# Signs of 64-bit weights masked as 32-bit words into a tile of marks, in an order made anew

## The chip, the cores and the metric

One core of a Trainium2 chip runs the whole program. The metric is its device time in microseconds (us). The engines are named as in the profile: PE (TensorE, matmuls), PEld (its weight loads), DVE (VectorE), ACT (ScalarE), POOL (GpSimd) and SP (SyncE, which issues the DMAs).

## What is computed

An attention with gates over 768 positions (2 batches, 8 heads of 40), as a recurrence; its output, 1536 tokens of 320, goes through a first layer with 64-bit weights, and then through 8 experts:

```
m_new = np.maximum(f_gate[:, :, t] + m, i_gate[:, :, t])
C = f_stab * C + i_stab * einsum('bhd,bhe->bhde', vt, kt)   # and n likewise
y[:, :, t] = o * (C q) / maximum(|n q|, 1)
...
h = x @ w_in                  # 320 x 2048, float64
g = np.maximum(0.01 * h, h)
x = (g @ w_out).astype(np.float32)     # 2048 x 320, float64
...
out += P[:, e:e + 1] * (np.maximum(x @ w1[e], 0.0) @ w2[e])   # 8 experts
```

## The kernel before

**Three stages.** The attention is worked in chunks of 128 positions with matmuls (six pairs, `c0` to `c5`, and more behind). The first layer runs over steps g: a block of 256 tokens by 128 hidden columns. Step g has an up product `u` (8 matmuls, L223), a leak `g` (ACT, L712), a rounded part `h` (ACT, L718), the remainder `l` (DVE, L723, tile `hla`) and a down product `d` (6 matmuls, L230 to L232). The experts follow.

**The 64-bit weights.** They arrive as pairs of 32-bit words and are turned into two fp32 parts on the chip. There are 16 loads n = 0 to 15: an even n is 768 columns of `w_in`, an odd n 640 columns of `w_out`. Each goes through these steps, named with their n: `L` the DMA (L158); `pa` the sign (L193, DVE): the top bit is taken from byte 7 of a pair and put in byte 3; `pl` three low bits (ACT L187 or DVE L185); `pu` a scaling of the high word (ACT L178 or DVE L176), which shifts the exponent's bias; `pb` the join (L199, DVE): the high word moved left by 3 and or-ed with the low word; `ph` the rounded part (ACT, L211); `px` the remainder, called a low here (L215, DVE or POOL). The raw words lie in four buffers: `rawU` for n % 4 = 3 and three `raws`, so load n+4 waits for the low of load n.

**What sets the order.** Up to the end of step 31 and the chunks c0 to c5, every engine's order is that of a table, `ORDER`: a list of task names that one loop runs through, each task issuing its instructions on its engines. `VECTORED` names the `pu` and `pl` that go to DVE instead of ACT, `POOLED` the tasks that go to POOL instead of DVE. Beside the steps the table has the chunks' tasks, `c1.xl` for instance: `bd` (L559) spreads the gates for a decay product, `ap0` and `ap1` are the decay products (L566, L568), `sc` the scores (L591), `wg` and `kw` weigh (L597, L602), `va` the values (L607), `zp` the product with the state (L613), `dp` the update of the state (L619) with its rows of decay (L475), `cr` carries it on (L660 to L665), `zt`, `ya`, `dn`, `sg`, `ou` make the chunk's output (L624 to L643), `tt`, `xi`, `xl` turn it into columns for PE (L335 to L345). `wN` stands for N dummy matmuls whose result isn't read (L881); 20 more of them run at the start (L899). The gates' scans (L412, L424) and what follows them (to L441) come first on DVE. From step 32 on, the order is that of the program's loops, and is not the table's.

Of the kernel before, what the change touches and what calls it, by code (L numbers as in the profile page):

```python
# [31 lines left out]
nT@0 c1.qP f2 ex c0.bd og0 pl3 L2 pu3 c2.q3 f4 w8@p c0.ap0@1 n8 c1.v c1.ap1@2 n5 f3 c1.kn w1@p c1.ap0@3 n9 c0.ex0 pa3  # L32
c0.ap1@1 n7 c0.sc c0.ex1 pb3 c1.ex0 c2.bd qT@1 c1.ex1 c0.wg pu1 pl1 w8@p c0.va@3 nS c0.kw ph3 pa1 qTe pl0 px3 c0.dp@2
pb1 pu0 c1.sc c0.cr nTe ph1 pa0 nL@1 px1 c2.ap1@0 nLe sg0 pb0 c3.ap1@2 L5 c2.kP c4.bd c0.dn c2.qP c1.wg c2.v c2.kn L7
pu2 c0.sg c3.kP c0.ou c2.ex1 c1.kw w13@h c0.tt@1 pl2 c1.va@3 qS pa2 c0.xi ph0 pb2 w3@h c1.dp@0 c3.ex1 px0 c0.xl pl5
c2.ap0@2 c1.cr qL@1 c2.ex0 c1.dn c2.zp@0 pu5 c1.sg L4 c2.kw c3.ap0@2 qLe c1.ou c3.q3 ph2 c2.zt c3.qP c1.tt@1 pa5 c3.kn
c2.sc@30 c1.xi px2 c3.ex0 c1.xl f6 w1@h c2.dp@2 c2.wg c4.kP u0 L6 c2.cr pu4 c2.va@1 c3.v pu7 pb5 g0 c4.ap0@0 h0 c3.kw
c2.ya u1 f5 l0 c2.dn c4.ap1@3 g1 d0 pl4 pl7 pa4 c3.zp@2 c4.ex0 h1 u2 c2.sg c4.q3 pu6 l1 c4.qP pb4 c3.sc@10 c4.v g2
c4.ex1 c4.kn pa7 ph4 u3 c2.ou h2 c3.wg px4 d1 g3 h3 l2 c3.dp@3 pl6 c2.tt@0 ph5 c4.kw L8 c3.va@1 c3.cr og4 c2.xi l3 u4
pa6 u5 c3.zt g4 pb7 d2 pb6 ph7 c4.zp@3 h4 px5 ph6 d3 px7 l4 L9 c2.xl g5 c4.dp@2 h5 c3.ya pu8 d4 px6 L11 pl8 c5.kn  # L40
c4.sc@01 c4.af c3.dn L10 sg4 l5 u6 c3.sg c4.wg c5.kP c5.qP d5 c5.q3 c3.ou pa8 u7 g6 pu11 c4.zt c3.tt@0 g7 c4.va@1
c3.xi h6 c3.xl h7 pl11 l6 pb8 c5.ap1@3 c5.v c5.ap0@0 c5.ex1 u8 l7 c4.ya d6 pa11 g8 u9 pu10 h8 pb11 ph8 d7 l8 c5.ex0
c4.dn c5.sc@13 g9 c4.sg e7 c5.af h9 u10 pl9 l9 c5.kw d8 ph11 px8 u11 px11 c5.wg c5.dp@0 g11 g10 d9 h11 L15 pl10 l11
L12 c5.va@1 c4.ou h10 pu9 l10 pa9 u12 pb9 c5.zp@3 pa10 g12 ph9 d10 h12 px9 u13 l12 L13 pu12 d11 g13 pb10 h13 d12 pu15
l13 pl15 ph10 u14 c5.zt px10 u15 g14 h14 L14 d13 l14 g15 f8 h15 u16 pa15 pl12 l15 pu13 d14 c5.ya g16 pb15 u17 h16 l16
c5.dn d15 g17 pl14 h17 u18 pu14 l17 c5.sg pa12 u19 g18 h18 pl13 d16 pb12 g19 l18 d17 h19 l19 u20 pa14 u21 pa13 g20
# [1262 lines left out]
```

## Time and profile before

| | |
|---|---|
| Time, median of 3 runs | 936.43 us (936.31 to 936.45) |
| The profiled execution | 936.21 us, of which the span is 934.5 |
| PE busy | 926.1 us, 99% of the span |
| DVE, ACT, POOL busy | 587.2, 490.3, 553.0 us |
| First up product (u0) begins | 33.40 us |
| First step behind the table (u32) begins | 112.23 us |

The span is the time from the profile's first instruction to its last; 1.7 us of the execution's time lie outside of it. Busy time of PE includes the dummy matmuls, and a matmul's duration includes its way through the array, so that those of successive ones overlap.

### The profile page before, as it was taken

The numbers are of one execution on the slowest core, as the hardware profiler recorded it, in microseconds if no ns is written. First come the engines' busy times: TensorE is split into PE (matmuls) and PEld (weight loads), VectorE is DVE, ScalarE is ACT, GpSimd is POOL, SyncE is SP. The second block draws the span as 40 slices with busy tenths as digits, with TensorE's granted clock in tenths as the row PEclk, the third lists the DMA queues.
The fourth block names the chain that finished last, engine by engine and source line by source line (L and its number), as shares of the span: only waits on it lengthen the run. The fifth ranks groups of instructions, "written<-read, shape, count | busy, mean of one in ns | idle before, by whom it ended". The sixth has DMA issues, their size and how long they took to land.

```text
span 934.5 us, 16892 instructions
## 1 busy us (share of the span) xinstructions
PE 926.1 (99%) x6192; PEld 904.7 (97%) x6192; DVE 587.2 (63%) x1179; ACT 490.3 (52%) x959; POOL 553.0 (59%) x575
## 2 busy tenths in 40 slices
...
GB/s 272 247 214 151 24 105 35 67 23 17 88 2 46 33 41 34 43 52 38 38 38 44 51 40 51 38 38 38 45 50 43 48 38 38 38 47 50 29 2 84
DMA packets 57384, 56.49 MB, mean 60 GB/s; under 512 B 7654, under 2 KB 48086, under 8 KB 57302
## 3 DMA queue, kind: packets, MB, share of 16 engines
...
q14 instruction: 34, 0.28, 0.1%
...
## 4 chain that ended last, share of the span: by engine, by line
PE 92%; DVE 3%; DMA 2%; ACT 1%; issue 1%; SPq 1%; POOL 0%; DVEq 0%; ACTq 0%
PE y L230 12%; PE y L231 12%; PE y L232 12%; PE ha L223 9%; PE b L1028 8%; PE b L1029 8%; PE b L1031 8%; PE b L1030 8%; PE ya L230 3%; PE ya L232 3%; PE ya L231 3%; PE yps L607 1%; PE sps L591 1%; PE zps L613 1%; DMA rawU<-in_w_out_dram 1%
## 5 line engine op out<-in xcount | busy, mean ns | idle before, releaser
L1052 POOL TENSOR_TENSOR hl<-c,hh 128x384 fp32r<-128x384 f32 x192 | 197.4, 1029 | 180.1 <-ACT c L1051 156.3
L230 PE MATMUL y<-w_e,hh 128*128 128x320 f32 x768 | 238.4, 310 | 0.0
L231 PE MATMUL y<-w_e,hh 128*128 128x320 f32 x768 | 236.9, 308 | 0.0
L232 PE MATMUL y<-w_e,hl 128*128 128x320 f32 x768 | 236.8, 308 | 0.0
L1110 DVE SCALAR_TENSOR_TENSOR acc<-y,Pg,acc 128x320 f32<-128x320 f32 x336 | 179.1, 547 | 63.6 <-PE y L232 56.3
L1050 ACT ACTIVATE hh<-c 128x384 fp32r<-128x384 f32 x192 | 99.8, 520 | 208.1 <-DVE c L1047 208.1
L1028 PE MATMUL b<-X,w_e 128*128 128x384 f32 x448 | 152.7, 341 | 0.2 <-DVE s L1068 0.2
L1029 PE MATMUL b<-X,w_e 128*128 128x384 f32 x448 | 151.0, 337 | 0.0
L1031 PE MATMUL b<-X,w_e 96*128 96x384 f32 x448 | 151.0, 337 | 0.0
L1030 PE MATMUL b<-X,w_e 128*128 128x384 f32 x448 | 150.8, 337 | 0.0
L230 PEld LDWEIGHTS y<-w_e,hh 128*128 128x128 f32 x768 | 144.2, 188 | 1.7 <-DVE acc L1108 1.1
L231 PEld LDWEIGHTS y<-w_e,hh 128*128 128x128 f32 x768 | 144.3, 188 | 0.0
L232 PEld LDWEIGHTS y<-w_e,hl 128*128 128x128 f32 x768 | 144.1, 188 | 0.0
L1051 ACT ACTIVATE c<-c 128x384 f32<-128x384 f32 x192 | 101.0, 526 | 18.0 <-ACT hh L1050 0.7
L223 PE MATMUL ha<-xT,w_a 128*128 128x256 f32 x768 | 109.2, 286 | 1.0 <-DVE hla L723 1.0
L1047 DVE TENSOR_TENSOR c<-b,s 128x384 f32<-128x384 f32 x192 | 100.6, 550 | 13.5 <-PE b L1031 10.1
L223 PEld LDWEIGHTS ha<-xT,w_a 128*128 128x128 f32 x768 | 101.0, 192 | 2.5 <-DVE hla L723 1.4
L1075 DVE SCALAR_TENSOR_TENSOR hl<-b,hh 128x384 fp32r<-128x384 f32 x64 | 35.6, 557 | 95.4 <-ACT hh L1074 95.4
L723 POOL TENSOR_TENSOR hla<-gg,hha 128x256 fp32r<-128x256 f32 x64 | 48.8, 763 | 78.0 <-ACT hha L718 71.0
L259 POOL TENSOR_TENSOR raw_e<-raw_e 128x256 f32<-128x256 f32 x116 | 85.1, 743 | 4.5
L1028 PEld LDWEIGHTS b<-X,w_e 128*128 128x128 f32 x448 | 84.8, 189 | 1.3 <-DVE s L1068 0.6
L1029 PEld LDWEIGHTS b<-X,w_e 128*128 128x128 f32 x448 | 85.2, 190 | 0.0
...
## 6 DMA issues: line engine op xcount, KB each, us to landing
...
rawU<-in_w_out_dram SPq DMA_DIRECT2D x4, 640.0 KB, 5.0
...
raws<-in_w_out_dram SPq DMA_DIRECT2D x4, 640.0 KB, 3.8
```

Source lines behind the costliest of these rows:

```text
L223: nc.tensor.matmul(h_ps, t1[:, ws, c * P:(c + 1) * P], xt[:, xs, t0:t0 + n], start=(j == 0), stop=(j == len(MM1) - 1),)
L230: nc.tensor.matmul(y_ps, a, t2[:, c, :], start=first, stop=False)
L231: nc.tensor.matmul(y_ps, a, t2[:, 2 + c, :], start=False, stop=False)
L232: nc.tensor.matmul(y_ps, b, t2[:, c, :], start=False, stop=last)
L1028: nc.tensor.matmul(bank, f[:, 0], b[:, 0], start=fresh, stop=False, skip_group_check=not fresh)
L1029: nc.tensor.matmul(bank, f[:, 0], b[:, 2], start=False, stop=False, skip_group_check=not fresh)
L1030: nc.tensor.matmul(bank, f[:, 2], b[:, 0], start=False, stop=False, skip_group_check=not fresh)
L1031: nc.tensor.matmul(bank, f[0:K3, 1], b[0:K3, 1], start=False, stop=True, skip_group_check=not fresh)
L1047: nc.vector.tensor_tensor(c, part, plus, op=ALU.add)
L1051: nc.scalar.activation(c, c, AF.Relu)
L1052: nc.gpsimd.tensor_tensor(hl[a][b], c, hh[a][b].bitcast(F32), op=ALU.subtract)
L1110: nc.vector.scalar_tensor_tensor(out=o, in0=y, scalar=Pg[:, 2 * HP * q + t, e:e + 1], in1=o, op0=ALU.mult, op1=ALU.add)
```

## The change

The sign is now an and of the whole high word with the top bit, from every second 32-bit word of the raw buffer into a contiguous tile of marks (`late`). The low bits are written behind it, as bytes into the lowest byte of each mark, so that `pa` stands ahead of `pl`, where `pl` stood ahead of `pa`. The join reads the marks in place of the low words. There is one tile of marks for even n and one for odd n, so the sign of load n+2 follows the join of load n. Two later uses share the memory of `late`: the leaked tiles of steps from 32 on, and the copies of `repeat`. Three steps that stood in the loops behind the table are now its last: `c6.bd`, `xr` (`repeat`) and `xl` (an expert's first load). `VECTORED`, `POOLED` and `ORDER` are new throughout; of `ORDER` the first line stands here.

```diff
-VECTORED = ('pl2', 'pl4', 'pu9', 'pu10', 'pu12', 'pl14', 'pl15')
-POOLED = ('c1.kw', 'c2.bd', 'c2.kw', 'c3.kw', 'c3.sg', 'c4.bd', 'c4.sg', 'px0', 'px2', 'px4', 'px7', 'px11')
+VECTORED = ('pu4', 'pu6', 'pu7', 'pl9', 'pu12', 'pu13', 'pl13', 'pu14')
+POOLED = ('c0.sg', 'c1.kw', 'c2.kw', 'c2.sg', 'c3.sg', 'c4.kw', 'c4.sg', 'c5.kw', 'c5.sg', 'px0', 'px4', 'px6', 'px7', 'px9', 'px11', 'px13', 'px14', 'px15')
...
-m0 gA gN gF rco a0 cst a1 a2 L3 n0 c0.kP a3 n1 a4 c0.kn n2 c0.qP f0 a6 L1 c0.v n4 im a9 a5 L0 a8 f1 n3 c1.kP n6 a7
+m0 L3 rco gA gN cst c1.kn gF pa3 L1 a0 c1.qP a1 n0 ex im pu3 a2 c0.kP n1 a3 pl3 c0.kn n2 og0 a5 a4 n3 c1.kP pb3 a6
...
         def bits(self, p, vector):
             if self.is64:
-                lw = self.raw[p][:, :, 0]
+                low, top = self.mark[p].bitcast(U8).rearrange("p (m t) -> p m t", t=4)[:, :, 0], self.octets(p)[:, :, 3]
                 if vector:
-                    nc.vector.tensor_scalar(out=lw, in0=lw, scalar1=29, scalar2=None, op0=ALU.logical_shift_right)
+                    nc.vector.tensor_scalar(out=low, in0=top, scalar1=5, scalar2=None, op0=ALU.logical_shift_right)
                 else:
-                    nc.scalar.activation(lw, self.octets(p)[:, :, 3], AF.Copy, scale=1.0 / 32, bias=-0.5 + 1.0 / 64)
+                    nc.scalar.activation(low, top, AF.Copy, scale=1.0 / 32, bias=-0.5 + 1.0 / 64)
         def sign(self, p):
             if self.is64:
-                b = self.octets(p)
-                nc.vector.tensor_scalar(out=b[:, :, 3], in0=b[:, :, 7], scalar1=0x80, scalar2=None, op0=ALU.bitwise_and)
+                self.mark[p] = marks[p][:, 0:(3 * UW, 2 * DM)[p]]
+                nc.vector.tensor_scalar(out=self.mark[p], in0=self.raw[p][:, :, 1], scalar1=-2 ** 31, scalar2=None, op0=ALU.bitwise_and)
         def join(self, p):
             if self.is64:
-                hw, lw = self.raw[p][:, :, 1], self.raw[p][:, :, 0]
-                nc.vector.scalar_tensor_tensor(out=hw, in0=hw, scalar=3, in1=lw, op0=ALU.logical_shift_left, op1=ALU.bitwise_or)
+                hw = self.raw[p][:, :, 1]
+                nc.vector.scalar_tensor_tensor(out=hw, in0=hw, scalar=3, in1=self.mark[p], op0=ALU.logical_shift_left, op1=ALU.bitwise_or)
...
+        late = ac.tile([P, 6 * BA], F32, tag="late", name="late")
+        marks[0:2] = [late[:, 0:3 * UW].bitcast(I32), late[:, 3 * UW:3 * UW + 2 * DM].bitcast(I32)]
...
-            x = h_ps[g] if g < TABLE else ha.tile([P, BA], F32, tag="gg", name=f"gg{g}", bufs=4)
+            x = h_ps[g] if g < TABLE else late[:, g % 4 * BA:(g % 4 + 1) * BA]
...
+        tasks["c6.bd"] = lambda: chunks[6].spread(chunks[7], engine("c6.bd"))
+        tasks["xr"] = lambda: x0[0].repeat(copy_rest)
+        tasks["xl"] = lambda: experts[0].load1(rawU.rearrange("p (n w) -> p n w", n=7))
```

**The order at three places.** DVE's first seven instructions before are a memset, the mask of the attention, and the gates' scans:

```order
L833 MEMSET R_76 128x369
L848 CAST mask<-R_76 128x128
L412 SCALAR_TENSOR_TENSOR sc_96<-sc_95 64x128
L417 COPY sc_95<-sc_95 64x1
L424 SCALAR_TENSOR_TENSOR sc_96<-sc_95 64x128
L412 SCALAR_TENSOR_TENSOR sc_96<-sc_95,sc_96 64x256
L428 TENSOR_TENSOR sc_96<-sc_96 64x128
```

After the change the sign of load 3 (`late<-rawU`) stands ahead of the scans, whose lines are now L420 and L432:

```order
L842 MEMSET R_76 128x369
L857 CAST mask<-R_76 128x128
L193 TENSOR_SCALAR late<-rawU 128x640
L420 SCALAR_TENSOR_TENSOR sc_93<-sc_92 64x128
L425 COPY sc_92<-sc_92 64x1
L420 SCALAR_TENSOR_TENSOR sc_93<-sc_92,sc_93 64x256
L432 SCALAR_TENSOR_TENSOR sc_93<-sc_92 64x128
```

The third row, the first of the signs, moved ahead of the first scan, and the second of the scans changed its place.

On DVE the rows up to `c1.xl`, the last that u0 reads, were before (L640 and L643 are `c1.sg` and `c1.ou`, L624 `c2.zt`, L344 and L345 `c1.xl`):

```order
L634 TENSOR_SCALAR den_397<-yps_359 128x8
L635 TENSOR_TENSOR den_397<-yps_359,den_397 128x8
L636 RECIPROCAL den_397<-den_397 128x8
L640 TENSOR_TENSOR R_76<-R_76,den_397 128x320
L643 TENSOR_TENSOR R_76<-yps_359,R_76 128x320
L624 TENSOR_TENSOR R_76<-zps_401,decT 128x328
L193 TENSOR_SCALAR raws_169<-raws_169 128x640
L344 TENSOR_TENSOR xT_370<-pt_a_419,xT_370 64x128
L345 TENSOR_TENSOR xT_370<-pt_a_419,xT_370 128x2x128
```

After the change `c1.sg` and `c1.ou` are L648 and L651, `c2.zt` is L632, and the rows ahead of them are those of loads 4 to 7 (L193, L176, L199, L215):

```order
L215 TENSOR_TENSOR w_a_385<-raws_156,w_a_385 128x640
L199 SCALAR_TENSOR_TENSOR rawU<-rawU,late 128x640
L176 TENSOR_SCALAR raws_185<-raws_185 128x768
L199 SCALAR_TENSOR_TENSOR raws_185<-raws_185,late 128x768
L648 TENSOR_TENSOR R_76<-R_76,den_403 128x320
L193 TENSOR_SCALAR late<-raws_199 128x768
L651 TENSOR_TENSOR R_76<-yps_360,R_76 128x320
L632 TENSOR_TENSOR R_76<-zps_416,decT 128x328
L344 TENSOR_TENSOR xT_407<-pt_a_389,xT_407 64x128
L345 TENSOR_TENSOR xT_407<-pt_a_389,xT_407 128x2x128
L344 TENSOR_TENSOR xT_407<-pt_a_449,xT_407 64x128
L345 TENSOR_TENSOR xT_407<-pt_a_449,xT_407 128x2x128
```

The last of the two turns is `c1.xl` in both; ahead of it `c0.xl` now stands directly (the first L344 and L345), and a low, two joins, a scale and a sign stand among the rows of chunk 1, where one sign stood (of `raws`, 128x640).

On PE the piece that ends just behind u0 (`ha`, L223) was before, from the last two of the eight score products of chunk 2 on (`sps_2`); `dps` is the update of that chunk and `yps` its values:

```order
L591 MATMUL sps_2_426<-R_76 128x128
L591 MATMUL sps_2_427<-R_76 128x128
L881 LDWEIGHTS R_76
L881 MATMUL w_443<-R_76 128x512
L619 MATMUL dps_445<-R_76 120x123 x3
L223 MATMUL ha_452<-xT_370,w_a_372 128x256 x8
L607 MATMUL yps_467<-R_76 128x41 x8
```

After the change the scores are L599, the rows of decay `dpc` L483, the update L627, the values L615 and the state product L621:

```order
L599 MATMUL sps_2_456<-R_76 128x128
L599 MATMUL sps_2_457<-R_76 128x128
L483 MATMUL dpc_472<-lastG,sc_92 120x6 x3
L627 MATMUL dps_479<-R_76 120x123 x3
L223 MATMUL ha_483<-xT_407,w_a_332 128x256 x8
L615 MATMUL yps_498<-R_76 128x41 x8
L621 MATMUL zps_510<-Cst_105,R_76 128x123 x3
```

In both the eight score products follow the turn `c1.tt` directly. The dummy between scores and update is gone; the rows of decay of chunk 2 (`dpc`, L475 before), which stood ahead of that turn, now stand there; and 12 dummies that aren't in this piece stand ahead of the turn.

## Rows read from the trace of the kernel before

**Rows 1.** The page, busy time and instructions of each engine.

```profile
PE 926.1 (99%) x6192; PEld 904.7 (97%) x6192; DVE 587.2 (63%) x1179; ACT 490.3 (52%) x959; POOL 553.0 (59%) x575
```

**Rows 2.** A stretch: busy time by engine, granted clock, DMA share, GB/s.

```profile
60.90:64.40 3.50, 3.50 (x17) 3.50 (x17) 3.47 (x8) 3.46 (x6) 0.00 (x0) 0.51 0.28 77
```

**Rows 3.** PE in order of time: start, duration, instruction, idle before it.

```profile
30.96 0.41 PE L335 MATMUL pt_a<-cst,R 128*128 128x128 f32 x2
...
31.52 1.16 PE L591 MATMUL sps<-R 40*128 40x128 f32 x16
...
33.40 1.19 PE L223 MATMUL ha<-xT,w_a 128*128 128x256 f32 x8
...
60.25 0.47 PE L566 MATMUL aps<-bd,stt 96*128 96x512 f32 x1 [1.12 <-DVE xT L345]
...
104.21 0.31 PE L230 MATMUL ya<-w_a,hha 128*128 128x320 f32 x1
...
105.09 1.12 PE L223 MATMUL ha<-xT,w_a 128*128 128x256 f32 x8
...
108.94 2.17 PE L223 MATMUL ha<-xT,w_a 128*128 128x256 f32 x16 [0.97 <-DVE hla L723]
...
112.23 1.21 PE L223 MATMUL ha<-xT,w_a 128*128 128x256 f32 x8
```

**Rows 4.** Groups by form, 0 to 240 us: busy, mean ns, idle.

```profile
L193 DVE TENSOR_SCALAR raws<-raws 128x768 uint8<-128x768 uint8 x8 | 8.3, 1041 | 0.1
L199 DVE SCALAR_TENSOR_TENSOR raws<-raws 128x768 int32<-128x768 int32 x8 | 7.6, 954 | 0.1
...
L193 DVE TENSOR_SCALAR raws<-raws 128x640 uint8<-128x640 uint8 x4 | 3.6, 901 | 0.0
...
L185 DVE TENSOR_SCALAR raws<-raws 128x768 int32<-128x768 int32 x3 | 1.6, 547 | 0.0
...
L559 DVE TENSOR_TENSOR bd<-mv,rco 64x1024 fp32r<-64x1024 f32 x1 | 1.2, 1187 | 0.0
```

**Rows 5.** DVE in order of time, ahead of u0.

```profile
3.24 0.42 DVE L412 TENSOR_TENSOR_SCAN sc<-sc 64x128 f32<-64x128 f32 x1 [0.55 <-DMA sc<-in_gates_dram]
...
7.84 0.70 DVE L441 SCALAR_TENSOR_TENSOR stt<-sc,rco,sc 32x128 fp32r<-32x128 f32 x2 [0.42 <-issue]
...
16.62 0.47 DVE L602 TENSOR_TENSOR R<-R 128x320 f32<-128x320 f32 x1
17.02 0.88 DVE L193 TENSOR_SCALAR raws<-raws 128x640 uint8<-128x640 uint8 x1
17.69 0.86 DVE L215 TENSOR_TENSOR w_a<-rawU,w_a 128x640 fp32r<-128x640 f32 x1
18.47 0.82 DVE L199 SCALAR_TENSOR_TENSOR raws<-raws 128x640 int32<-128x640 int32 x1
...
32.46 0.42 DVE L345 TENSOR_TENSOR xT<-pt_a,xT 128x256 fp32r<-128x256 f32 x1
```

**Rows 6.** A DVE instruction and the POOL instruction beside it.

```profile
44.17 1.17 DVE L602 TENSOR_TENSOR R<-R 128x320 f32<-128x320 f32 x1 [0.40 <-PE dps L619]
...
43.12 1.86 POOL L215 TENSOR_TENSOR w_a<-raws,w_a 128x768 fp32r<-128x768 f32 x1 [6.21 <-ACT w_a L211]
```

**Rows 7.** DMA issues, 0 to 130 us: count, KB, median us to landing.

```profile
raws<-in_w_out_dram SPq DMA_DIRECT2D x4, 640.0 KB, 3.8
```

**Rows 8.** The chain that ended last, 0 to 66 us: start, us, what.

```profile
0.81 0.66 SPq L397
...
29.15 0.53 PE dpc L475 x6
...
33.01 0.63 PE dps L619 x6
...
34.59 1.71 PE yps L607 x16
...
38.69 0.67 PE zps L613 x6
```

More of the change, by code (lines that the diff above doesn't have):

```diff
@@ L32 @@
[L32 to L46, printed above, removed]
@@ L47 @@
-ph12 pb13 d18 h20 g21 l20 d19 h21 pb14 ph15 u22 l21 e19 u23 g22 h22 ph13 d20 l22 wl px12 g23 d21 h23 ph14 l23 u24 px14
-d22 g24 h24 u25 l24 px15 u26 g25 px13 d23 c5.ou g26 h25 h26 d24 l25 l26 f9 c5.tt@3 u27 c4.tt@1 g27 u28 h27 l27 f7 d25
-g28 c5.cr c4.xi u29 d26 c4.xl g29 h28 h29 d27 l28 l29 u30 e27 u31 g30 c5.xi h30 d28 ws c5.xl g31 h31 l30 l31 c4.cr
+m0 L3 rco gA gN cst c1.kn gF pa3 L1 a0 c1.qP a1 n0 ex im pu3 a2 c0.kP n1 a3 pl3 c0.kn n2 og0 a5 a4 n3 c1.kP pb3 a6
+c0.qP a7 L0 ph3 n4 c1.v a8 n5 pa1 c0.v nS c0.bd L2 pu1 pl1 f0 w17@p c0.ap0@0 n6 nL@1 pb1 c0.ap1@2 c0.ex0 f1 nT@3 n7
@@ new lines @@
+c0.ex1 n8 ph1 f2 sg0 px1 a9 L5 f4 w10@p c1.ap1@0 px3 c1.sc nLe f3 n9 c1.ap0@2 c0.kw c0.sc pa0 c1.ex1 c2.bd c1.ex0
+c0.dp@1 pl0 c2.qP c0.wg c2.ap1@0 c1.kw pu0 c3.kn f6 pb0 w4@h c0.va@2 c3.qP L7 c0.cr nTe c2.q3 ph0 pa2 qT@3 pa5 pu2
+c1.dp@1 px0 c0.dn pl2 c1.wg pu5 pb2 c2.ex1 L4 c2.kn pl5 c1.va@0 c0.sg c1.cr c2.kP ph2 qS c2.v pb5 qTe c0.ou f5 px2
+c2.ap0@1 ph5 pa7 L6 c0.tt@3 pu7 og4 c2.ex0 pa4 pl7 c3.ap0@2 c2.kw c1.dn c0.xi px5 c3.ap1@1 c3.ex0 pb7 pl4 c2.zp@2 pu4
+c3.ex1 pb4 ph7 c3.q3 c1.sg c3.kP ph4 pa6 c4.kn c1.ou c3.v px4 c2.zt w12@h c1.tt@1 c0.xl c2.sc@02 c1.xi sg4 c1.xl px7
@@ new lines @@
+L8 qL@3 c2.wg L9 c2.dp@1 u0 pu6 pl6 c2.cr c2.va@0 g0 qLe c4.bd c3.zp@2 c4.v pb6 c4.ap0@1 c4.q3 c4.ap1@3 u1 L11 c4.ex1
+c2.ya c4.qP pa8 h0 c3.sc@03 ph6 c4.kP f8 l0 c4.ex0 px6 u2 pu8 c3.wg d0 g1 g2 f7 h2 L10 c3.va@1 c4.af h1 c2.dn pl8 l1
+c3.kw c2.sg l2 c3.dp@0 c2.ou u3 pa11 c3.zt d1 g3 c3.ya pu11 c3.cr u4 h3 pl11 c4.sc@32 pb8 l3 d2 c5.qP pa10 c5.kP c3.dn
+c5.ap1@1 pu10 c4.zp@0 c4.wg c3.sg ph8 u5 c4.kw px8 c5.ap0@2 c5.kn g5 c4.va@3 g4 L12 h4 h5 l4 pb11 u6 c5.ex1 c3.ou pl10
+l5 d3 c4.zt g6 pb10 c3.tt@1 h6 c5.ex0 c4.dp@0 pa9 c3.xi l6 u7 c5.v c5.kw c4.ya pa12 c5.sc@23 g7 c5.af c3.xl ph10
@@ new lines @@
+c2.tt@1 ph11 px10 d4 c2.xi px11 pl12 d5 c2.xl pu9 u8 pl9 L15 h7 c5.q3 d6 l7 g8 L14 f9 h8 d7 pu12 l8 c5.wg c5.dp@1 u9
+pb9 c5.va@2 ph9 pa15 g9 px9 h9 u10 e7 l9 c4.dn pb12 u11 L13 c4.sg c5.zp@3 g11 g10 d8 h10 h11 l10 d9 pu15 l11 c4.ou u12
+u13 g12 h12 ph12 d10 l12 c5.zt g13 u14 px12 h13 pl15 l13 d11 pa14 g14 pb15 pl14 d12 pu14 h14 u15 l14 pa13 u16 c5.ya
+g15 pb14 h15 ph15 d13 pu13 g16 l15 d14 h16 l16 u17 c5.dn pl13 d15 g17 c5.sg h17 d16 ph14 c5.ou l17 u18 c6.bd u19 px14
+g18 h18 d17 l18 g19 h19 u20 px15 l19 wl d18 g20 h20 u21 l20 pb13 d19 g21 h21 u22 l21 e19 u23 g22 ph13 d20 g23 px13 h22
@@ L50 @@
+h23 d21 l22 l23 d22 c5.cr u24 u25 g24 h24 d23 l24 g25 h25 u26 l25 d24 g26 h26 c4.tt@3 l26 u27 c5.tt@2 g27 u28 h27 l27
+d25 g28 c4.xi d26 h28 c4.xl l28 u29 ws d27 g29 h29 u30 c5.xi l29 e27 u31 g30 h30 d28 l30 g31 c5.xl h31 l31 c4.cr xr xl
 """
@@ L127, in mlstm_moe_kernel @@
     wide = w_in.dtype == mybir.dt.int64
-    raws, homes = {}, {}
+    raws, homes, marks = {}, {}, []
     class Banks:
@@ L145, in __init__ @@
             self.i, self.src, self.nm, self.is64 = i, (w1_ap, w2_ap), nm, is64
-            self.t, self.raw = [None, None], [None, None]
+            self.t, self.raw, self.mark = [None, None], [None, None], [None, None]
         def load(self, p):
@@ L358, in mlstm_moe_kernel @@
         wv = st1.enter_context(tc.tile_pool(name="wv", bufs=1))
-        rrp = st1.enter_context(tc.tile_pool(name="rrp", bufs=1))
         ha = st1.enter_context(tc.tile_pool(name="ha", bufs=5))
```

11 lines of the change are left out of this document (8 added, 3 removed).

## The prediction

> **What bounds the kernel now.** I read the page's first line, then TensorE (PE) in order of time up to the end of the table, then VectorE (DVE) over the same stretch. The page says PE is busy 926.1 of 934.5 us [rows 1]. So an edit to DVE, ScalarE (ACT) or GpSimd (POOL) work is worth only what it takes out of PE's gaps, of the dummy matmuls ahead of the first real ones, and of time at a low clock. Everything from step 32 on is the same program in both kernels and PE is saturated there, so I compare one moment: the start of `up(32)`, here u32, 112.23 us in the profile before [rows 3]. The forecast is its own time, 936.2 (934.5 of span and 1.7 outside), moved by what u32 moves; the median 936.43 is 0.2 above it, and that difference I leave out.
>
> Two parts lie ahead of u32. **The front**, up to u0 (33.40, [rows 3]): PE waits there for the attention chunks and fills up with dummies, and DVE sets the pace: `c1.xl`, the last of what u0 reads, ends at 32.88 [rows 5], half a microsecond ahead of u0. **The body**, u0 to u32: 78.8 us. Three losses show in it: a decay matmul 1.12 late (queued behind a late load), the half-speed stretch that follows (granted 0.51, so TensorE at 1.2 instead of 2.4 GHz, for 3.5 us: 1.7 lost [rows 2]), and 0.97 at 108 where a step waits for an `hla` of DVE [rows 3]. Without them it would be 75.0. From prices per step it is less. An up step is 1.12 long, of which the last 0.16 lies under the next, as a down matmul is 0.31 long but the next one starts 0.147 later: 0.96 and 6 x 0.147 = 0.88 [rows 3]. So 32 x 0.96 + 29 x 0.88 = 56.2; four value steps at 1.71, three state products at 0.67, three updates at 0.63 [rows 8], three score steps at 1.10, four turns at 0.56 (30.96 to 31.52), and four decay matmuls of 0.47 of which half is hidden [rows 3] add 17.2. Sum 73.4. The body is then 73.4 to 75.0 when nothing stands still.
>
> **The change, part by part.**
> *The sign.* Before, a byte operation: 1041 ns at 768 columns, 901 at 640. What it becomes, a 32-bit mask with a constant, strided in and contiguous out, isn't in the trace; the nearest row is the 32-bit shift at L185 with a constant, 547 ns at 768, and by columns some 480 at 640 [rows 4]. Bounds: 0.48/0.55 and no gain at all (0.90/1.04). I take the lower end, as width of element and kind of operation are alike. Durations overstate the gain: the byte sign at 17.02 took 0.88 but the next started 0.67 later, whereas other operations overlap some 0.07 (17.69, 0.86, next at 18.47) [rows 5]. By spacing a sign goes from 0.82 to 0.50 or 0.67 to 0.42, and 16 of them save 8 x 0.32 + 8 x 0.25 = 4.6 us of DVE, spread over 112.
> *Bits and join.* The bits keep their engines' prices: the ACT form is a byte read with a wider write in both. The join reads contiguous marks rather than every second word; with two operands from memory it took 954 and 822 [rows 4, 5], and I take the same. In the two bits on DVE the byte form returns (0.3 each; both behind u0, where DVE isn't last).
> *One marks tile per part.* The sign of load n+2 now waits for the join of load n, in order on DVE, so that costs nothing by itself; but bits on ACT stand between a sign and its join, and DVE queues behind that join if ACT is late.
> *Order ahead of u0.* This is the large term. Up to `c1.xl` the new DVE list holds 8 signs, 7 joins, 4 lows and 2 `bd` against 5, 4, 2 and 1, two scales more, one bits and one `sg` fewer. By spacing: signs 4 x 0.50 + 4 x 0.42 = 3.7 against 4.2 (-0.5); joins 4 x 0.75 + 3 x 0.88 = 5.6 against 3.4 (+2.2); lows +1.6 (0.78 at 640 [rows 5], 0.88 at 768); scales +0.9, priced as the shift; `bd` +1.1 [rows 4]; bits and `sg` -1.0. Sum +4.3.
> *The first instructions.* Load 3 now goes first on SP's queue and its sign is third on DVE, ahead of the first scan, which ran at 3.24 [rows 5]. Load 3 is 640 KB; such a load took 3.8 from issue to landing [rows 7], and the queue's first transfer went out at about 0.8, so the scans start near 4.6: +1.4. The gates' own first transfer moves from first to third on that queue, where an issue takes 0.66 [rows 8], so 1.2 of it is there even if load 3 lands at once. Two short idles on DVE ahead of `c1.xl`, the first at 7.84 [rows 5], of 0.42 and 0.43, can take up 0.85, so I take +0.5, with bounds of 0.3 and 1.4.
> So `c1.xl` ends at 32.9 + 4.3 + 0.5 = 37.7 and `c1.ou`, which stands five instructions ahead of it (0.5 for one and 0.3 to 0.4 for four), some 1.8 earlier, at 35.9. PE then has a turn 0.56, scores of chunk 2 1.10, its decay row 0.53 [rows 8], its update 0.63: u0 at 38.7. Bounds 37.7 (the PE steps overlap as the matmuls in them do) and 39.4 (the start at its upper bound).
> *Dummies, POOL and late steps.* Nine more dummies only fill PE's waits there. POOL gets nine lows for five (+4 x 1.9) and loses `c2.bd` and `c4.bd` to DVE (the second is behind u0); it was busy 59% [rows 1] and waited for ACT. The three steps moved into the table's end (`c6.bd`, `xr`, `xl`) were issued a few steps later before; they feed work 4 steps on, and a `bd` of 1.2 to 1.9 beside four steps of 1.8 is hidden. If it weren't, it would show as a PE gap behind u36.
> **The sum.** u32 = 38.7 + 73.4 = 112.1 against 112.23, so 936.2 - 0.1 = **936.1**. What PE waits longer in front it gets back behind: with seven loads joined before u0 where four were, DVE has nine of 16 left to join, and none of the three losses needs to recur. With the body at 75.0 it is 937.7, with u0 at 37.7 it is 935.1.
>
> **A rule against it.** When POOL was in a low of 1.86 (43.12 to 44.98), a DVE multiplication that reads two operands from memory and takes 0.47 otherwise (16.62, [rows 5]) stood 1.17, and ended 0.36 after POOL did [rows 6]: they exclude each other. No row shows a single-operand DVE instruction held up so. The Trainium skill, page "SBUF — State Buffer", section "SBUF: two separate sides", says that VectorE and GpSimd share a port pair as an exclusive lock, that the one that starts first keeps it for the whole instruction, and that on VectorE's side also one-operand instructions in a two-port mode take it. By that rule the new 32-bit sign would meet POOL's lows, where the byte sign perhaps did not; the sum by the rule would be that of the third case below.
>
> **The rivals.**
> *A: front and body cancel*, 935.1 to 937.7, as summed.
> *B: faster; the front's extra work falls into waits.* DVE's list ahead of u0 doesn't pack as I add it: the load in front costs nothing, and an instruction more stands where DVE would have waited for PE. u0 at 36.5 and a body of 73.4 give u32 at 109.9: 933.9 (933.0 to 934.5). For it: the three losses, 3.8 us, are of the old order's making. Against it: DVE was nearly without idle in front, so 4.3 us of work need 4.3 us. In the extreme the whole 4.6 of DVE time comes out: 931.6.
> *C: slower; POOL holds up the signs or joins.* The first low on POOL (`px0`, 1.9) comes in the table between the signs of loads 2 and 5 and the join of load 2. If it starts just ahead of one of them, all behind it on DVE moves by up to 1.9, `c1.xl` and u0 too: 938.0; with the next low (`px4` or `px6`) as well 939.9, or 939.7 where PE's wait costs 1.7 of low clock again. It decides from the second hit on, or from one hit with the clock. Against: a DVE instruction that comes first makes POOL wait instead, and POOL has time.
> *D: the sign isn't cheaper.* If the stride or the width undoes it, eight signs ahead of u0 cost 4 x 0.32 + 4 x 0.25 = 2.3 more: 938.4.
>
> **How the numbers follow.** A measurement here tells 0.2% (1.9 us) from no change. A 0.48 (all of it within), B 0.32 with its extreme at 0.02 of that, C 0.16, D 0.04. So faster 0.32, same 0.48, slower 0.20. The time is A's, 936.1. The range, 933.2 to 938.8, holds A, most of B and the single hit of C; it leaves out B's lowest end, C with two hits and part of D, under 0.2. A's own range is 935.1 to 937.7.
>
> **What would show it.** Right: L193 at about 0.55 and 0.48; u0 between 37.7 and 39.4, with more dummy time ahead; after it no granted clock near 0.5 and no PE wait over 0.5 up to u32; u32 within 111.1 to 113.7. Wrong: u0 before 37.5 (B); DVE instructions of double length ending just behind a POOL low (C); L193 near 1 us (D); a PE wait behind u32 for something that the table's end now issues; or `pb` on DVE idle for bits from ACT, which I priced at nothing.

## The result, and the profile after

The changed kernel takes 941.95 us (940.92 to 943.49, 3 runs) against 936.43, a ratio of 1.0058 with a 95% interval of 1.0044 to 1.0072: 5.5 us slower, above the range of 933.2 to 938.8, where 936.1 had been forecast. Its profiled execution is the shortest of the three, 940.92, with a span of 938.3. In a second set of six it took 940.95 to 948.06, where the kernel before took 936.02 to 937.26; so the change has also made the time vary (in the later sets the kernel before went from 935.56 to 940.26).

Two of the page's lines, busy time and what the DMA engines did in 40 slices:

```profile
PE 928.1 (99%) x6201; PEld 905.1 (96%) x6201; DVE 580.8 (62%) x1175; ACT 491.8 (52%) x958; POOL 557.3 (59%) x580
...
DMA  9853030200201011111111111111111111111002
```

PE is still busy 99%, DVE 6 us less than in [rows 1]. That says nothing on the result; the time is in the first 40 us. DVE in order of time there:

```profile
5.85 0.49 DVE L193 TENSOR_SCALAR late<-rawU 128x640 int32<-128x640 int32 x1 [3.15 <-DMA rawU<-in_w_out_dram]
6.37 0.42 DVE L420 TENSOR_TENSOR_SCAN sc<-sc 64x128 f32<-64x128 f32 x1
...
26.79 1.51 DVE L199 SCALAR_TENSOR_TENSOR raws<-raws,late 128x768 int32<-128x768 int32 x1
...
31.67 0.55 DVE L193 TENSOR_SCALAR late<-raws 128x768 int32<-128x768 int32 x1
...
36.56 0.48 DVE L651 TENSOR_TENSOR R<-yps,R 128x320 f32<-128x320 f32 x1
...
38.69 0.42 DVE L345 TENSOR_TENSOR xT<-pt_a,xT 128x256 fp32r<-128x256 f32 x1
```

The mask took 0.49 and 0.55 (31.67), where 0.48 and 0.55 had been forecast. But the first scan began at 6.37, where [rows 5] has 3.24, and `c1.xl` (38.69) ended at 39.11, 6.2 later than before. From the sign of load 3 (5.85) to the end of `c1.xl` DVE stood only 0.17: 33.1 us of work, where the kernel before has 28.8 from its first scan to there. That is the +4.3 of the prediction's list, though 0.6 of it is one join (26.79) that took 1.51 instead of 0.95. What released the first scan, in the chain of waits (start, us, what):

```profile
0.81 0.39 SPq L158
...
1.25 0.55 SPq L856
...
1.85 4.50 DMA sc<-in_gates_dram
...
6.37 0.43 DVE sc L420
```

The gates' first transfer, 64 KB, was issued third at 1.85 and took 4.50, where it took 2.4 in the kernel before: it landed at 6.35, behind the 640 KB of load 3 at 5.8. The sign of load 3 ended at the same moment, 6.34, so in this trace either of the two was enough to hold the scan to 6.37. The prediction had taken 4.6 for the scan's start. PE in the same trace, first up to u0, then to u32:

```profile
27.76 1.98 PE L615 MATMUL yps<-vt_odd,Pm_odd 128*128 128x41 f32 x16 [1.75 <-ACT R L581]
...
37.19 0.41 PE L335 MATMUL pt_a<-cst,R 128*128 128x128 f32 x2 [0.44 <-DVE R L651]
...
40.13 1.20 PE L223 MATMUL ha<-xT,w_a 128*128 128x256 f32 x8
...
51.11 0.86 PE L627 MATMUL dps<-vt_odd,R 128*120 128x123 f32 x6 [1.07 <-DVE R L610]
```

```profile
115.46 0.28 PE L223 MATMUL ha<-xT,w_a 128*128 128x256 f32 x1
...
124.83 1.12 PE L223 MATMUL ha<-xT,w_a 128*128 128x256 f32 x8
```

u0 is at 40.13, 6.73 later than in [rows 3]. The table issues u32 at another place among the down matmuls, so u36 is the better mark: 124.83, where the kernel before has 121.15. The body up to there is 84.70 long instead of 87.75, so 3.05 of the 6.73 came back, and not the 5.4 of the prediction. One wait of 1.07 (51.11) stands in it, for a weighing on DVE (L610). The chain of waits leads to it through DVE instructions that stood beside POOL's (DVE, then POOL):

```profile
48.32 1.05 DVE L642 TENSOR_SCALAR den<-R 128x8 f32<-128x8 f32 x1
...
56.05 0.17 DVE L642 TENSOR_SCALAR den<-R 128x8 f32<-128x8 f32 x1
```

```profile
47.94 1.41 POOL L584 TENSOR_SCALAR_AFFINE_SELECT R<-R 128x1024 f32<-128x1024 f32 x1
49.89 0.72 POOL L648 TENSOR_TENSOR R<-R,den 128x320 f32<-128x320 f32 x1 [0.55 <-DVE den L644]
```

The first of them took 1.05 where the same instruction takes 0.17 at 56.05, and ended 0.02 after POOL's (49.35). The weighing, at 50.02, took 0.95 where it takes 0.49 elsewhere, and ended 0.36 after POOL's next (50.61). That is 1.3 in all, more than the wait. The wait is there with 1.05 to 1.07 in five of the new order's other traces too.

The last 0.3 comes later: the turn of the copies that `xr` makes (129.41) takes 0.68 to the next up step, where the turn at 126.67 takes 0.35, and u40 is 4.0 late. The span is 3.8 longer.

After PE's stand of 1.75 at 26, TensorE's clock fell to its lower level (columns as in [rows 2]; the clock is the third figure from the end):

```profile
25.90:29.90 4.00, 2.25 (x20) 1.98 (x18) 4.00 (x8) 4.00 (x8) 1.58 (x2) 0.99 0.98 352
29.90:33.40 3.50, 3.43 (x11) 1.94 (x11) 3.40 (x9) 3.50 (x8) 0.86 (x1) 0.52 0.98 338
33.40:37.20 3.80, 3.36 (x19) 1.70 (x19) 3.70 (x8) 2.79 (x4) 0.39 (x1) 1.00 1.01 347
```

In this execution it costs nothing, since PE waited for `c1.ou` at 37.19 anyway. The other two executions, the median among them, are 1.0 and 2.6 longer, with a mean granted clock of 0.994 where this one has 0.998.

### The profile page after: what moved, and what is told of

Its sections match the earlier page's. It is cut to its first block, busy times and chain, and to the rows that moved or that the text cites. A ratio compares the mean times of both kernels' runs of the same rounds, so it can differ in the third digit from the quotient of the medians.

```text
span 938.3 us, 16921 instructions
## 1 busy us (share of the span) xinstructions
PE 928.1 (99%) x6201; PEld 905.1 (96%) x6201; DVE 580.8 (62%) x1175; ACT 491.8 (52%) x958; POOL 557.3 (59%) x580
## 4 chain that ended last, share of the span: by engine, by line
PE 95%; DVE 3%; ACT 1%; DMA 0%; issue 0%; SPq 0%; DVEq 0%; ACTq 0%
PE y L230 12%; PE y L231 12%; PE y L232 12%; PE ha L223 10%; PE b L1040 8%; PE b L1041 8%; PE b L1043 8%; PE b L1042 8%; PE ya L230 3%; PE ya L232 3%; PE ya L231 3%; PE yps L615 2%; PE sps L599 1%; PE zps L621 1%; PE dps L627 1%; PE aps L574 1%
## 5 line engine op out<-in xcount | busy, mean ns | idle before, releaser
L223 PE MATMUL ha<-xT,w_a 128*128 128x256 f32 x768 | 108.3, 285 | 0.1
L223 PEld LDWEIGHTS ha<-xT,w_a 128*128 128x128 f32 x768 | 100.1, 190 | 1.2 <-ACT late L720 0.3
L731 POOL TENSOR_TENSOR hla<-late,hha 128x256 fp32r<-128x256 f32 x64 | 49.3, 771 | 86.8 <-ACT hha L726 61.3
```

Of the source, the lines that this page charges most:

```text
L223: nc.tensor.matmul(h_ps, t1[:, ws, c * P:(c + 1) * P], xt[:, xs, t0:t0 + n], start=(j == 0), stop=(j == len(MM1) - 1),)
```

## The experiments

u0 is the start of the first up product in each profiled execution; "before" is the kernel before on the same chip. The tables' ratios are to that.

**The changed kernel again, and the start.** The first is the same kernel. The second puts the gates ahead of load 3 again, the third leaves load 3 first and only moves its sign, and the fourth is the kernel before with load 3 put first and nothing else:

```diff
 e2:  -m0 L3 rco gA gN cst c1.kn gF pa3 L1 a0   +m0 gA gN gF rco cst c1.kn L3 L1 a0 ... n2 pa3 og0 a5 pu3 a4 pl3 ... a6 pb3
 e3:  -gF pa3 L1 a0 c1.qP a1 n0 ex im pu3       +gF L1 a0 c1.qP a1 n0 ex im pa3 pu3
 e15: -m0 gA gN gF rco a0 cst a1 a2 L3          +m0 L3 gA gN gF rco a0 cst a1 a2      (order of before)
```

Expected: the kernel again: 

> The changed kernel once more, for its spread and a second trace. Both theories: 941 to 943.5, with the first scan near 6.4 and u0 near 40.1. If the loss is only in the front, executions differ by what the clock does: where more than the 3.5 us after 29.9 are at half speed, the time is 1 to 2.5 above the fastest. If the spread is not the clock, it shows at a mean clock of 0.998 too.


Gates first: 

> The changed kernel with the gates' loads and the constants ahead of load 3 again, and sign, scale and bits of load 3 some tasks later. Theory 1 (the front is late because the first scan starts 3.1 late and DVE has no idle to give it back): first scan near 3.3, u0 near 37.5 to 38, time 2 to 3 below the changed kernel, 938.5 to 940. Theory 2 (the number of DVE instructions ahead of u0 sets it, the start is absorbed): u0 within 0.7 of 40.1, time above 940.5.


Sign later: 

> The changed kernel with load 3 still first on the queue, but its sign behind the first two scans. If the sign's wait holds up the scans (the step of the prediction), the first scan comes at about 4.5 and u0 about 1.5 earlier: 939.5 to 941. If the gates' own transfers land late behind the bytes of load 3, the first scan stays near 6.3 and the time within 1 of the changed kernel.


Load first in the kernel before: 

> The kernel before with one change: load 3 goes first on the queue, ahead of the gates. Theory (the gates behind a load of 640 KB land some 3 late and DVE has little idle to give back): first scan at 5.6 to 6.4, u0 2 to 3 later, 938.5 to 939.5. Rival (the front absorbs it): within 1 of the kernel before.

| | median (range) us | ratio (95%) | first scan | u0 |
|---|---|---|---|---|
| changed kernel again | 942.99 (940.95 to 948.06) | 1.0077 (1.0058 to 1.0097) | 5.97 | 45.86 |
| gates first | 945.42 (943.44 to 947.94) | 1.0094 (1.0080 to 1.0108) | 3.13 | 44.68 |
| load first, sign later | 943.16 (940.84 to 951.22) | 1.0087 (1.0056 to 1.0119) | 6.21 | 46.85 |
| kernel before, load first | 940.88 (939.64 to 942.02) | 1.0044 (1.0031 to 1.0057) | 6.35 | 35.90 |

The last line tells most. One name moved in the old order costs 4.0 us (2.9 to 5.3 by the interval). Its first scan (from DVE in order of time) and the two transfers (issues: count, KB, median us to landing):

```profile
6.35 0.42 DVE L412 TENSOR_TENSOR_SCAN sc<-sc 64x128 f32<-64x128 f32 x1 [3.65 <-DMA sc<-in_gates_dram]
```

```profile
rawU<-in_w_out_dram SPq DMA_DIRECT2D x1, 640.0 KB, 5.2
...
sc<-in_gates_dram SPq DMA_DIRECT2D x1, 64.0 KB, 5.1
```

The 64 KB took 5.1 behind the 640 KB. u0 came 2.5 later, and u32 3.4 later (115.61 in its trace). With the sign later the scan starts at 6.21 all the same: the gates' own transfer is late enough by itself, without DVE's queue behind the sign, which the prediction had priced. Gates first mends the scan (3.13) but not the new order, since that order needs load 3 early: DVE stood 2.67 for that load and 1.14 for its bits, both ahead of `c0.bd`, for which PE stood 3.0.

The trace of the changed kernel's second set, of its longest execution (948.06), shows where the time can go. DVE and POOL in order of time, and the granted clock by stretch:

```profile
12.11 0.49 DVE L193 TENSOR_SCALAR late<-raws 128x640 int32<-128x640 int32 x1 [1.55 <-DMA raws<-in_w_out_dram]
...
37.99 1.95 DVE L193 TENSOR_SCALAR late<-raws 128x768 int32<-128x768 int32 x1 [0.93 <-DMA raws<-in_w_in_dram]
39.86 0.48 DVE L651 TENSOR_TENSOR R<-yps,R 128x320 f32<-128x320 f32 x1
```

```profile
37.68 1.84 POOL L215 TENSOR_TENSOR w_a<-raws,w_a 128x768 fp32r<-128x768 f32 x1 [3.98 <-ACT w_a L211]
39.48 1.89 POOL L215 TENSOR_TENSOR w_a<-rawU,w_a 128x640 fp32r<-128x640 f32 x1
```

```profile
30.00:33.50 3.50, 3.50 (x17) 2.65 (x16) 3.40 (x9) 3.50 (x8) 0.53 (x1) 0.55 0.98 370
33.50:40.50 7.00, 4.30 (x21) 1.99 (x21) 5.96 (x9) 3.98 (x7) 3.02 (x3) 0.98 0.97 295
40.50:47.50 7.00, 7.00 (x40) 6.39 (x41) 4.67 (x12) 4.02 (x4) 0.87 (x1) 0.51 0.64 225
47.50:57.50 10.00, 8.96 (x80) 8.50 (x79) 8.77 (x16) 6.97 (x13) 3.99 (x3) 1.00 0.66 212
57.50:61.00 3.50, 3.46 (x16) 3.50 (x17) 3.36 (x10) 0.29 (x2) 0.00 (x0) 0.53 0.15 61
```

Load 1 landed at 12.0 instead of 10.7 and DVE stood 1.55 for it ahead of `c0.bd` (12.11). Load 6 landed late too, and its sign, which the order put ahead of `c1.ou` (39.86), stood 0.93 for the load and then 1.95 long instead of 0.55, until 0.42 after POOL's low (37.68 to 39.52): the one-operand mask is held up by POOL as the two-operand instruction of [rows 6] was. That agrees with the rule of the Trainium skill, page "SBUF — State Buffer", section "SBUF: two separate sides", that a DVE instruction in a two-port mode, and not only one with two SBUF inputs, shuts out GpSimd and is shut out by it for a whole instruction. The trace doesn't show the mode. PE then stood 2.41 for `c1.ou`, fell to the lower level again at 40.5 for 7 us and at 57.5 for 3.5, and did u0 and the work around it there: u0 at 45.86. The three traces of over 950 us (sign later, and below sign 1 behind `c0.bd` and 8 dummies more) have the same place: the sign of load 6 stood 0.94, 1.32 and 1.37 for its load and took 1.92, 1.57 and 1.51, and PE stood 3.7, 2.9 and 2.7 for `c1.ou`. Over the six executions the time goes with the mean granted clock: 940.95 at 0.998, 941.6 to 943.5 at 0.994, 945.5 and 948.1 at 0.991 and 0.992. The expectation had given the clock 1 to 2.5; the longest is 7.1 above the shortest.

**The mask by itself.** The old order with the new sign, the bits directly behind it (e4) or the sign moved ahead to its bits (e10); then the same as e10 with load 3 (e16) or all five loads ahead of u0 (e17) done in the old way. And the new order with the old sign (e5):

```diff
 e4:  -pl3 L2 pu3 ... c0.ex0 pa3        +L2 pu3 ... c0.ex0 pa3 pl3     (so for each n)
 e10: -pl3 L2 pu3 ... c0.ex0 pa3        +pa3 pl3 L2 pu3 ... c0.ex0     (but not for n = 14)
 e16: +BYTES = (3,)      e17: +BYTES = (3, 1, 0, 2, 5)
+            if self.is64 and 2 * self.i + p in BYTES:
+                ...     (bits, sign and join of the kernel before, bits first)
 e5:  bits, sign and join of the kernel before; -pa3 L1 ... pu3 ... pl3   +L1 ... pu3 ... pl3 pa3
```

Bits behind: 

> The masks and marks alone in the order of before (each bits task moved directly behind its sign, the three late steps back in the loops, engines assigned as before). Theory 1 (the mask itself is a gain and the new order the loss): u0 1 to 2 earlier than before, near 32, and the time 934 to 936.5. Rival (bits that must wait for the sign make ScalarE and then the joins late): u0 at 33.5 or later and 937 or more.


Sign ahead: 

> The masks and marks in the order of before once more, but with each sign put directly ahead of its bits (that of load 14 alone stays where it was), so that the bits on ScalarE wait less than 14.5 us in all as they did with the bits behind the sign's old place. Theory (the mask is a gain of 0.3 an instruction, and what the old order lost was ScalarE waiting for signs): 934.5 to 937. Rival (the 32-bit sign and its marks cost in this order too, by waits for POOL or for loads): 939 or more.


Load 3 old: 

> The old order with signs ahead of their bits, but load 3 in the old way (bits first, byte sign), since ScalarE stood 1.6 there for the sign. Theory (a wait of ScalarE for a sign is what the mask costs at the start): u0 near 33.5 instead of 35.3, time 936 to 937.5 in a set where the kernel before gives 936.5. Rival (u0 late by other causes): u0 at 35 or more, time as with all loads new, 1.5 to 2 above the kernel before.


Five loads old: 

> The same with all five loads whose signs stand ahead of u0 in the old order (3, 1, 0, 2, 5) in the old way, and the eleven others with mask and marks. Theory: the front is that of the kernel before (u0 33.2 to 33.6), and behind it DVE has 0.3 less per sign, so 934.5 to 936.5. Rival (behind u0 the waits of ScalarE for signs cost as much as the masks save): 936.5 to 939.


New order, old sign: 

> The new order with the old byte sign, the bits ahead of it and the join from the low word again (each sign moved directly behind its bits). If the 32-bit sign pays where it stands: 8 signs ahead of u0 cost 0.25 to 0.32 more each, u0 2 later than in the changed kernel at the same clock, time 943 to 946. Rival (what the mark saves is lost on waits for POOL and for bits): time within 1.5 of the changed kernel's, and no byte sign of double length beside a low on POOL.

| | median (range) us | ratio (95%) | u0 | ScalarE's wait for signs, 0 to 120 us |
|---|---|---|---|---|
| old order, bits behind | 941.64 (941.47 to 941.85) | 1.0055 (1.0043 to 1.0067) | 35.59 | 14.5, 10 times |
| old order, sign ahead | 939.40 (938.72 to 940.91) | 1.0022 (1.0012 to 1.0032) | 35.28 | 8.2, 7 times |
| and load 3 old | 938.23 (937.44 to 939.23) | 1.0016 (1.0007 to 1.0025) | 34.96 | 7.8, 7 times |
| and all five old | 937.33 (935.87 to 938.77) | 1.0002 (0.9993 to 1.0011) | 33.37 | 6.0, 5 times |
| new order, old sign | 956.70 (953.63 to 957.20) | 1.0215 (1.0202 to 1.0228) | 45.99 | |

Sixteen signs that are each 0.4 to 0.5 shorter when nothing holds them up make the old order slower, by 2.0 (1.1 to 3.0) with all of them and the sign ahead. ScalarE's waits in the old order with the sign ahead (us in total, times, longest), and the first of them in order of time:

```profile
ACT late L187 <- DVE late L193: 8.2, 7, 2.0
```

```profile
11.75 0.93 ACT L187 ACTIVATE late<-rawU 128x640 uint8<-128x640 uint8 x1 [1.60 <-DVE late L193]
```

The bits of load 3 ran at 9.94 in the kernel before, when DVE was busy with the gates. Now they need its sign, which DVE gives at 11.7, and everything behind them on ScalarE, the exponentials of chunk 0 too, moves. So this is what a mark costs in front: a new wait of ScalarE for DVE. The bits on ScalarE are dearer as well, 0.94 and 1.09 in this trace where they took 0.80 and 0.93. With all five loads ahead of u0 done in the old way the front is as before (33.37), and the eleven masks behind it gain nothing that can be measured (ratio 1.0002): one of them (44.41) took 1.70 beside a low of POOL, on the chain to a wait of PE of 0.70 (48.25), and ScalarE waits another 6.0. These runs keep the shared memory of `late`, which by that ratio costs nothing that shows.

My expectation of load 3 alone fell (u0 at 34.96, not 33.5). In that trace POOL stands beside two of the four new signs ahead of u0; the second (DVE, then POOL):

```profile
28.55 1.69 DVE L203 TENSOR_SCALAR late<-raws 128x640 int32<-128x640 int32 x1
```

```profile
28.04 1.85 POOL L226 TENSOR_TENSOR w_a<-raws,w_a 128x768 fp32r<-128x768 f32 x1 [2.23 <-ACT w_a L222]
```

It ended 0.35 after the low, and the first, 0.98 long at 16.22, 0.35 after POOL's `bd` (16.85). The turn of `c0` is 0.8 later than before and u0 1.6, so the second half came while this sign was held up. How much of the five loads' cost is the wait for signs and how much is POOL isn't separated. The new order with the old sign is far worse than either kernel: the bits must then be done first, and DVE stands 7.5 for them in the first 120 us; that order was made for the mask.

**What the new order prepares ahead of u0.** Five kernels move signs or add dummies, and two take the preparation of loads 4, 6 and 7 behind `c1.xl` and u0:

```diff
 e9:  -c3.kP ph4 pa6 c4.kn ... c1.xl            +c3.kP ph4 c4.kn ... c1.xl pa6
 e11: -n5 pa1 c0.v nS c0.bd L2                  +n5 c0.v nS c0.bd pa1 L2
 e12: both of them
 e13: both of them, on e2, and                  -a6 pb3 ... L0 ph3     +c0.bd pa1 pb3 ph3 L2
 e8:  -pl5 c1.va@0                              +pl5 w8@h c1.va@0
 e7:  pa4 pl4 pu4 pb4 ph4 px4, the same of load 7, px5, pa6, L8 and L9 from ahead of c1.tt to around u0; -w12@h +w4@h
 e14: the same, with pu6 pl6 pb6 ph6 px6, pa8 and pu8, spread over steps 0 to 2, behind c4.bd
```

Sign of load 6: 

> The changed kernel with one instruction moved: the sign of load 6, which stands ahead of c1.ou on DVE and there waits for its load and for the low on POOL, behind c1.xl. Theory 1 (this wait makes the slow executions): spread below 1.5 and median 940 to 941, u0 near 39.6 in the profile. Rival (the spread comes from the loads and the clock in general): spread of 3 or more and median above 941.5.


Sign of load 1: 

> The changed kernel with one instruction moved: the sign of load 1, which DVE reaches at 10.5 and which stood 1.5 to 1.65 idle in most traces because that load lands at 10.7 to 12.4, behind c0.bd, which PE waits for. Theory (this wait and PE's idle time behind it make the difference between 941 and the later executions): c0.bd 1 to 1.5 earlier where load 1 lands at 12, median 940 to 942. Rival (the queue's loads are late as a whole, and only the place of the wait moves): median 942.5 to 945.


Both: 

> Both moved: the sign of load 1 behind c0.bd and that of load 6 behind c1.xl. Theory of waits for loads on DVE: 939 to 941 and a spread below 2. Rival as for the one before: 942.5 or more.


All three: 

> The gates ahead of load 3 on the queue, the sign, join and rounding of load 3 and the sign of load 1 behind c0.bd, the sign of load 6 behind c1.xl. Theory (all of the front's loss is DVE standing behind loads): first scan near 3.2, c0.bd 2 earlier, u0 36.5 to 38.5, 937 to 939.5. Rival (later work of the list is late by then, as with the gates first alone): 942 or more.

 In this kernel the sign of load 1 overwrites the marks of load 3 ahead of the join that reads them, so that part of the weights differs. The sign of load 3 also stayed ahead of `c0.bd`, other than expected: DVE stood 5.15 for that load (11.32) and PE 4.5 for `c0.bd`. So this run doesn't test what it was made for.
Dummies: 

> The changed kernel with 8 more dummies ahead of the values of c1, where PE stood idle 1.75 at 25.9 and fell to half speed after it. If that idle time brings the half speed: no such stretch near 30, the other executions' added stretches fewer, median 940 to 941.5. Rival (the fall has another cause or costs nothing there): half speed near 30 as before, median 941.5 to 943.5.


Lighter front: 

> The changed kernel with 10 DVE instructions (signs of loads 4, 6, 7, their scales and joins, the low of load 5) and what follows them taken from ahead of c1.xl to behind it and u0, and 4 in place of 12 dummies ahead of that turn. Theory 1 (DVE's list ahead of u0 sets u0): u0 near 35 to 36.5 and 936 to 939, and no execution with more than one or two stretches at half speed. Rival (ScalarE and PE set it as well, and the body loses what the front gains): u0 at 38 or later, or time within 1.5 of the changed kernel's.


Once more: 

> The changed kernel with the preparation of loads 4 to 8 taken behind u0 once more, now spread over steps 0 to 2 and behind c4.bd, which PE waited 8.4 for when it stood behind the whole block. Theory (the number of weights prepared ahead of u0 is the loss): u0 36 to 39 and the body without a wait over 2, so 937 to 940.5. Rival (ScalarE and the loads set the front, or the body then lacks the weights): 942 or more.

| | median (range) us | ratio (95%) | u0 |
|---|---|---|---|
| sign 6 behind `c1.xl` | 944.53 (942.94 to 945.18) | 1.0080 (1.0068 to 1.0092) | 43.22 |
| sign 1 behind `c0.bd` | 943.94 (941.62 to 951.48) | 1.0076 (1.0049 to 1.0103) | 47.79 |
| both | 946.93 (942.92 to 950.69) | 1.0094 (1.0072 to 1.0117) | 44.20 |
| both, gates first | 946.79 (946.43 to 947.08) | 1.0098 (1.0085 to 1.0112) | 47.05 |
| 8 dummies more | 946.91 (942.38 to 951.08) | 1.0108 (1.0085 to 1.0131) | 45.61 |
| lighter front | 948.50 (948.02 to 950.76) | 1.0131 (1.0118 to 1.0144) | 39.12 |
| lighter front, spread | 946.33 (945.66 to 947.80) | 1.0106 (1.0092 to 1.0120) | 40.25 |

None of them helps. All seven theories fell; in six the rival's time or u0 came, and with the dummies neither did. No single sign makes the loss: where one no longer waits, the next thing does. With the sign of load 6 moved the times lie within 2.2, but the median is no lower, and with both signs moved they spread over 7.8. The dummies kept the clock at its upper level behind `c1.va`, but in the profiled execution PE stood 2.7 for `c1.ou` at 41.5, and the clock was at the lower level from 43 to 60.5. Only the lighter fronts bring u0 below 41, and their waits show that the body then waits for what was taken out or for what stands behind it, as `c4.bd` does in the first (waits of PE: us in total, times, longest):

```profile
PE aps L574 <- DVE bd L567: 10.3, 2, 8.4
PE yps L615 <- ACT R L581: 1.8, 1, 1.8
```

```profile
PE yps L615 <- ACT R L581: 2.7, 2, 1.7
PE aps L574 <- DVE bd L567: 2.0, 1, 2.0
PE dps L627 <- DVE R L610: 1.8, 1, 1.8
PE sps L599 <- DVE R L637: 1.6, 1, 1.6
```

u0 stays at 39 to 40 even there. The chain of waits of the second lighter front shows what holds it:

```profile
15.69 0.60 ACT R L581
...
28.17 0.49 ACT R L581
...
28.70 2.51 PE yps L615 x16
...
39.76 0.75 PE dps L627 x6
```

From 15.69 to 28.66 it is ScalarE, which has the exponentials behind bits and scales, and from there to u0 PE itself, without a wait but with a granted clock of 0.50 from 30 to 36. PE stands 1.7 to 1.8 for `R` of L581 ahead of `c1.va` in four of these seven traces, both lighter fronts among them, as in the changed kernel (27.76).

**A stand of PE, and the lower clock.** The kernel before, with ScalarE's scaling and bits of load 11 moved behind the turn of `c3`; and the same with masks on loads 6 and 9 to 15 alone:

```diff
 e18: -g6 pu11 c4.zt c3.tt@0 g7 c4.va@1 c3.xi h6 c3.xl h7 pl11 l6    +g6 c4.zt c3.tt@0 g7 c4.va@1 c3.xi h6 c3.xl h7 pu11 l6 pl11
 e19: the same, +BYTES = (3, 1, 0, 2, 5, 7, 4, 8)
```

The move alone: 

> The kernel before with the scaling and the bits of load 11 on ScalarE moved behind the turn of c3 and the rounding of step 7, so that ScalarE's wait of 1.7 for that load no longer holds up the turn. Theory (PE's stand of 1.1 and the 3.5 us at half speed behind it cost 2.8): no such stretch near 60, 933.5 to 935.5. Rival (the stand moves to the next thing that ScalarE owes, or DVE is behind it anyway): within 1 of the kernel before.


With eight masks: 

> The same move, with the mask and marks for loads 6 and 9 to 15 alone and the old way for the eight loads ahead. Theory (masks save DVE time where the bits' wait for the sign is covered, and DVE sets the steps behind 60): 0.5 to 1.5 below the kernel with the move alone, 932.5 to 934.5. Rival (DVE isn't on the path there): the same time as with the move alone, within 0.7.

933.53 (932.96 to 935.19), ratio 0.9969 (0.9959 to 0.9980), and 934.17 (933.81 to 935.94), ratio 0.9977 (0.9967 to 0.9986). The first is 2.8 below the kernel before and the fastest of all; the masks add nothing to it, and in their trace PE stands 0.7 more for `hla`. The stretch of [rows 2] in its trace, and the waits of PE up to 260 us:

```profile
60.90:64.40 3.50, 3.50 (x35) 3.19 (x34) 1.89 (x6) 3.47 (x10) 1.31 (x2) 1.00 0.14 41
```

```profile
PE ha L223 <- DVE hla L723: 1.0, 1, 1.0
```

The clock is 1.00 where it was 0.51, the stand of 1.12 is gone, and the 0.97 at `hla` is left. 1.1 and 1.7 is the 2.8 that the prediction had read from the rows for these two, so here both the stand and the stretch behind it were on the path.

## Why the prediction was wrong

*The sum.* The profiled execution is 4.8 above the forecast. Of that 1.4 is u0 (40.13 instead of 38.7), 1.9 the body to u32 (75.3 instead of the 73.4 in the sum), 0.6 what comes behind u32, and 0.9 lies outside the span (2.6 instead of 1.7), where no trace tells the cause; the next two executions have 1.7 there, but longer spans.

*The sign and the list ahead of u0* came out: 0.49 and 0.55, and 4.3 us more of DVE work up to `c1.xl` (33.1 against 28.8). The second is partly luck. By the prediction's own spacings the old list's five signs and four joins are 3.7 and 3.3, not 4.2 and 3.4, and the sum is 5.0; and 0.6 of the measured 4.3 is the join that took 1.51.

*The first instructions* was the step that failed. It priced load 3's place at +0.5, from a landing at 4.6 and two idles that would take up part. Load 3 landed at 5.8 and the gates at 6.35. The sign of load 3 so began 2.6 later than the first scan did before (5.85 against 3.24); less the 0.7 of idles that vanished this is 1.9, and the 1.4 above the price is all that u0 was late against the forecast. Put first in the kernel before, the same load costs 4.0. The 3.8 for the load came from other loads; its own transfer had taken 4.3 in the kernel before (issues, 0 to 12 us), and took 5.0 here:

```profile
rawU<-in_w_out_dram SPq DMA_DIRECT2D x1, 640.0 KB, 4.3
```

And the gates were moved by their place in the queue alone (1.2), with the time of their transfer (2.4) as it was, although it now shared the DMA engines with 640 KB.

*The body* was the second: the forecast had 5.4 come back in it, and 3.05 did. It was taken at 73.4 to 75.0, with no stand in it. It was 75.3 to u32, of which 1.07 and 0.25 are waits; without them 74.0, so the price by steps was 0.6 low. "None of the three losses needs to recur": a stand of another kind came, and the lower clock did recur, in front, without cost in the profiled execution, and at cost in others.

*Bits and join*: the joins kept their durations where POOL didn't hold them up. The bits on ScalarE didn't keep theirs (0.92 and 1.09 instead of 0.80 and 0.93), and the prediction priced their new order at nothing. In the old order sign, bits and their order together cost 1.1 to 3.0, with ScalarE waiting for signs; the prediction named a wait at the bits as a thing that would make it wrong, without a price. That the new order pays this price by putting load 3 first, so that its sign and bits come early, is read from the two orders and not shown by a run: gates first in the new order was worse.

*The rival C* (POOL holds up signs or joins) was right as a mechanism, and its reach was taken too small. In front the join at 26.79 stood 1.51 instead of 0.95 beside POOL's `px0` and what follows it, which gave 0.6. In the body, where the prediction had no place for it, it lies on the chain to the 1.07 wait of PE. Where a load was late the sign of load 6 took up to 1.95, 1.4 more. That POOL is the cause is read from where these instructions end; no run took POOL's instructions away. *The late steps* cost 0.3 at u40 and not nothing.

What is left open: how much of the loss beside the load is the eight signs and seven joins ahead of u0, how much is POOL, and how much the lower clock. The lighter fronts brought u0 down, but lost it in the body, so the price of that block by itself isn't settled; and 4.0 for the load and 2.0 for the marks were measured in the old order, where that they add up to about the 5.5 may be chance.
